# The first K block's transposes recorded ahead of the constants, and a planner that knows what large GpSimd loads cost to issue

## The chip, the core and the metric

The kernel runs on one core of one Trainium2 chip. The core has TensorE (PE, matrix products and transposes, with LDWEIGHTS shown as PEld), VectorE (DVE), ScalarE (ACT) and GpSimd (POOL); SyncE (SP) only issues DMAs here. Each engine works through its own instructions in program order and waits at semaphores for the others. The metric is the device time of one execution in microseconds. The time before is the median of 6 runs.

## The reference

The forward pass is a gated block: a layer norm, a long convolution along the sequence by an FFT, and a gated feed-forward part. The kernel returns the output and the gradients of all nine differentiable inputs.

```python
B, S, D = 1, 2048, 512        # F = 1376, shift kernel of 4 taps, bfloat16
def _fwd_reference(A_q, A_k, A_v, A_shift_k, A_ssm_k, A_ssm_D, B_x, B_w_gate, B_w_up, B_w_down):
    def _A_ref(q, k, v, shift_k, ssm_k, ssm_D):
        ...
        for t in range(ks):
            k_shift = k_shift + k_pad[:, t:t + S, :] * shift_k[:, ks - 1 - t][None, None, :]
        kv = k_shift * v
        ...
        y_f = kv_f * kf_f[None, :, :, :]        # FFTs of kv and of ssm_k, length 2 S
        y = irfft2(y_f) ...
        y = y + kv * ssm_D[None, None, :]
        return q * y
    def _B_ref(x, w_gate, w_up, w_down):
        g = jnp.einsum("bsd,df->bsf", x, w_gate)
        u = jnp.einsum("bsd,df->bsf", x, w_up)
        h = _sigmoid(g) * u
        return jnp.einsum("bsf,fd->bsd", h, w_down)
    x = A_q
    xn = _layernorm(x, axis=-1)
    s = _A_ref(xn, A_k, A_v, A_shift_k, A_ssm_k, A_ssm_D)
    g = _silu(_B_ref(xn, B_w_gate, B_w_up, B_w_down))
    return x + s * g

def reference(...):
    ...
    _out, _vjp = jax.vjp(_f, A_q, A_k, A_v, A_shift_k, A_ssm_k, A_ssm_D, B_w_gate, B_w_up, B_w_down)
    _grads = _vjp(grad_out)
```

## The kernel before

The kernel doesn't issue its instructions as it is written. `kernel_impl` calls a recorder, class `Rec`: each operation becomes a record with a running number, its dependencies worked out from the memory that it reads and writes. `Rec.order` then plans all of them with a list scheduler over a model of the machine, and `Rec.emit` (line 519, the line that the profile names for nearly everything) issues them in the planned order. In the plan each engine takes, among the records that are ready in the model, the one with the lowest number. So the place where an operation is recorded is its priority. An operation recorded with `evac` may go to ACT or to DVE, whichever the planner finds free (lines 421 to 428 and 245); it copies a PSUM tile to SBUF. The order on every engine is fixed once it is planned: if reality is later than the model, the engine waits.

Times in the model come from `cost` for engines and from `dcost` (line 331) for DMAs. `dcost` returns two numbers: how long the issuing engine is held (0.56 us for a DMA issued on POOL, 0.4 for others) and the transfer's duration, from its bytes and its shortest contiguous run. `run`, worked out in lines 338 to 346, is that run in bytes. DMAs on POOL go through software there (SWDGE), those on SP through hardware.

Four streams of work run together in the first 170 us, merged by `run_streams` (line 998): `strG`, the gate and up products of the feed-forward part, tile by tile over 16 tiles of 128 tokens; `strK`, the transform of the convolution kernel; `strV`, the shift convolution and the transform of kv; `strX`, their product and the inverse transform. K, V and X each work on four blocks (`cg`) of 128 channels. Then come the feed-forward backward pass (`stepB`), the weight gradients (`dW`) and the convolution's backward pass (`frontC`, `backC`).

The change touches the head of this. In lines 805 to 847 are recorded, in this order: the loads of the taps and of the first tile x (`ld_x`), the first K block (`ld_KT(0)`, 512 KB on SP), the weights, two more x tiles, and the k and v blocks (`ld_kv`, two loads of 512 KB on POOL for each block, in runs of 256 bytes); the column `Dcol_b` of the D taps, loaded on ACT; the broadcast of the shift taps; the identity matrix; `f_ln(SEQ[0])`, the layer norm of the first tile (statistics and a normalisation, with a power of -0.5 on POOL between); and `gen_fft_consts` (line 549), which makes the cosine tables: integer arithmetic on DVE, then three Sin on ACT, the two large ones into the halves of `Cf`, one for small tables. `f_ln(SEQ[1])` comes behind it.

`strK` (line 915) does four things for a block: it adds the D tap to column 0 of the block `KT` (one 128x1 addition on DVE), transposes `KT` in 16 pieces of 128x128 on PE into two PSUM tiles, copies each of these to `KC` (1024 columns, ACT or DVE), and then runs `step1`: products of the cosine table `Cf` with `KC`. `KT_r`, the buffer of the K block, exists once, so the load of the next block waits for the transposes. `gen_ci` transposes the cosine table itself, 32 pieces in four tiles. PSUM tiles of transposes come from banks 4 to 7 (`trA`), those of products from pairs of the eight banks (`mm2`), so they share banks.

In the V stream the accumulator `acc` (line 941) has one buffer too: four multiplications and three additions of 2048 columns on DVE fill it, it is stored to `ksh_d` by a DMA on POOL (line 953), multiplied by v, and the next block can overwrite it when the store has landed.

Of the kernel before, what the change touches and what calls it, by code (L numbers as in the profile page):

```python
# [9 lines left out]
ALU = mybir.AluOpType  # L10
# [9 lines left out]
S = 2048  # L20
# [144 lines left out]
def esize(dt):  # L165
    return 4 if dt in (f32, i32) else 2
# [16 lines left out]
class Rec:  # L183
# [147 lines left out]
    def dcost(self, alt):  # L331

        eng, meth, a, k = alt
        dst, src = a[0], a[1]
        nb = math.prod(dst.shape) * esize(dst.dtype)
        if "transpose" in meth:
            return nb / 260e3, nb / 170e3
        run = 1 << 20
        for v in (dst, src):
            dims = [d for d in v.ap if d[1] > 1]  # L340
            r = 1
            for s, n in reversed(dims if str(v.space) == "DRAM" else [d for d in v.ap[1:] if d[1] > 1]):
                if s != r:
                    break
                r *= n
            run = min(run, r * esize(v.dtype))
        if eng == "gpsimd" and run >= 256:
            run = 1024
        rate = 340e3 if run >= 2048 else 290e3 if run >= 1024 else 250e3 if run >= 512 else 150e3 if run >= 256 else run * 500
        par = dst.shape[0] if str(dst.space) != "DRAM" else src.shape[0]  # L350
        d = nb / rate
        if par < 16:
            d = min(d * 16, d + 1.0)
        return (0.56 if eng == "gpsimd" else 0.4), d

    def order(self):
        import heapq
# [185 lines left out]
def make_identity(nc, ident):  # L543
    nc.gpsimd.memset(ident, 0.0)
    nc.gpsimd.affine_select(out=ident, in_=ident, compare_op=ALU.not_equal, fill=1.0,
                            base=0, pattern=[[-1, ident.shape[1]]], channel_multiplier=1)
# [69 lines left out]
def kernel_impl(ctx, tc, A_q, A_k, A_v, A_shift_k, A_ssm_k, A_ssm_D, B_x, B_w_gate, B_w_up, B_w_down,  # L616
                grad_out, out_0, out_1, out_2, out_3, out_4, out_5, out_6, out_7, out_8, out_9):
    nc = tc.nc
# [26 lines left out]
    def ps_tr(shape, dt=bf16, name=None):  # L645
        return nc.ps(PS["tr"], shape, dt)

    ident = Ring(ar, [P]).ap
# [4 lines left out]
    Dcol_b = Ring(ar, [NG]).ap  # L653
# [42 lines left out]
    def f_ln(i, part=None):  # L696
        xj = T[i]["xq"]
        if part == 1:
            f_ln2(i)
            return  # L700
        st = T[i]["st"] = lnst.next()
        nc.vector.bn_stats(st[:, 0:6], xj)
        nc.vector.bn_aggr(st[:, 6:8], st[:, 0:6])
        nc.vector.tensor_scalar_add(st[:, 8:9], st[:, 7:8], LN_EPS)
        nc.gpsimd.tensor_tensor(out=rstd_all[:, i:i + 1], in0=st[:, 8:9], in1=neghalf, op=ALU.pow)
        if part is None:
            f_ln2(i)

    def f_ln2(i):
        xj, st = T[i]["xq"], T[i]["st"]  # L710
        nc.vector.scalar_tensor_tensor(nmr_all[:, i:i + 1], st[:, 6:7], -1.0, rstd_all[:, i:i + 1], ALU.mult, ALU.mult)
        r, b = rstd_all[:, i:i + 1], nmr_all[:, i:i + 1]
        nc.add([("scalar", "activation", (xnA[:, i, :], xj, ACT.Identity), dict(bias=b, scale=r)),
                ("vector", "tensor_scalar", (xnA[:, i, :], xj, r, b, ALU.mult, ALU.add), {})])
# [54 lines left out]
    KC_r = Ring(ar, [NJ, GW])  # L769
# [9 lines left out]
    stA = {}  # L779

    def ld_KT(cg):
        stA["KT", cg] = KT_r.next()
        nc.sync.dma_start(stA["KT", cg], A_ssm_k[cg * GW:(cg + 1) * GW, :])
# [53 lines left out]
        nc.scalar.copy(skb[:, :, db * 128:(db + 1) * 128], pb[:].rearrange("p (d t) -> p t d", t=4))  # L837
    make_identity(nc, ident)
    f_ln(SEQ[0])
    nc.gpsimd.memset(wg[:, :, F:FP], 0.0)  # L840
    nc.gpsimd.memset(wu[:, :, F:FP], 0.0)
    gen_fft_consts(nc, ar, ia, ib, negpi, Cf, BD, R)
# [21 lines left out]
    def step1(src, Qg):  # L864
        for jb in range(2):
            for c in range(2):
                ps = ps_mm([8, GW], name="ps_q")
                for jj in range(8):
                    j = jb * 8 + jj
                    nc.tensor.matmul(ps[:, jj, :], Cf[:, c, j, :], src(j), start=True, stop=True)  # L870
                nc.evac(Qg[:, c, jb * 8:(jb + 1) * 8], ps[:].rearrange("p j (g e) -> p j e g", e=4), 1024)
                yield 1024

    def flip(Qg, Qf):
        for gb in range(GQ // 8):
            pt = ps_tr([8, 128], name="ps_fl")
            for gi in range(8):
                g = gb * 8 + gi
                nc.tensor.transpose(pt[:, gi, :], Qg.rearrange("p c j e g -> p (c j e) g")[:, :, g], ident)
            nc.evac(Qf[:, gb * 8:(gb + 1) * 8, :], pt[:], 1024)  # L880
            yield 1024
# [33 lines left out]
    def strK():  # L915
        for cg in range(NG):
            KT = stA.pop(("KT", cg))
            nc.vector.tensor_tensor(KT[:, 0:1], KT[:, 0:1], Dcol_b[:, cg:cg + 1], ALU.add)
            KC = KC_r.next()
            for jh in range(2):  # L920
                pt = ps_tr([8, 128], name="ps_kt")
                for jj in range(8):
                    nc.tensor.transpose(pt[:, jj, :], KT[:, 8 * jh + jj:S:16], ident)
                nc.evac(KC[:, 8 * jh:8 * jh + 8, :], pt[:], 1024)
                yield 1024
            if cg + 1 < NG:
                ld_KT(cg + 1)
            Qg = QgK_r.next()
            yield from step1(lambda j: KC[:, j, :], Qg)
            while cg > 1 and ("s3K", cg - 2) not in flags:  # L930
                yield 0
            Qf = QfK_r.next()
            yield from flip(Qg, Qf)
            stA["QfK", cg] = Qf
            flags.add(("flK", cg))
# [32 lines left out]
    def strX():  # L968
        yield from gen_ci()
        for cg in range(NG):  # L970
# [13 lines left out]
            for qq in range(5):  # L984
# [9 lines left out]
                if qq > 0:  # L994
                    yield from inv3(ys.pop(qq - 1), qq - 1, Bg)
            yield from inv1(Bg, y2A[:, :, cg * GW:(cg + 1) * GW])

    run_streams([(gG, len(FA) * 11776, 0.05, 0.7), (strK(), 4 * 10240, 0.0, 0.7), (strV(), 4 * 16384, 0.0, 0.8),
                 (strX(), 4 * 24576 + 4096, 0.2, 1.0)])
    for r in (KT_r, KC_r, kh_r, vg_r, acc_r, term_r, kvt_r, QgK_r, QgV_r, QfK_r, QfV_r, KFg_r, Bg_r, Xc_r, Xs_r, Y_r, Ci_r):  # L1000
# [43 lines left out]
    for dst, w in ((wgT, wg), (wuT, wu)):  # L1044
        for fb in range(0, NFB, 2):
            nb = min(2, NFB - fb)
# [351 lines left out]
@with_exitstack  # L1398
def kernel(
    ctx: ExitStack,  # L1400
    tc: tile.TileContext,
    A_q: bass.AP,
    A_k: bass.AP,
    A_v: bass.AP,
    A_shift_k: bass.AP,
    A_ssm_k: bass.AP,
    A_ssm_D: bass.AP,
    B_x: bass.AP,
    B_w_gate: bass.AP,
    B_w_up: bass.AP,  # L1410
    B_w_down: bass.AP,
    grad_out: bass.AP,
    out_0: bass.AP,
    out_1: bass.AP,
    out_2: bass.AP,
    out_3: bass.AP,
    out_4: bass.AP,
    out_5: bass.AP,
    out_6: bass.AP,
    out_7: bass.AP,  # L1420
    out_8: bass.AP,
    out_9: bass.AP,
):
    kernel_impl(tc, A_q, A_k, A_v, A_shift_k, A_ssm_k, A_ssm_D, B_x, B_w_gate, B_w_up, B_w_down,
                grad_out, out_0, out_1, out_2, out_3, out_4, out_5, out_6, out_7, out_8, out_9)
# [30 lines left out]
```

## Time and profile before

| | us |
|---|---|
| median of 6 runs | 548.98 (548.06 to 552.69) |
| the profiled execution | 548.91 |
| its span, first to last instruction | 547.1 |
| PE busy | 524.1 |
| DVE busy | 457.1 |
| ACT busy | 347.1 |
| POOL busy | 150.7 |

The span is smaller than the time by 1.8 us, which lie outside the first and last instruction. An engine's busy time is the union of its instructions. PE's matmuls are pipelined and their ends are modelled. A name such as `slab<-psum` gives what an instruction writes and what it reads; `slab` is the one SBUF buffer in which everything lies, so shapes tell the operations apart. "128x1 bf16" is the D-tap addition, "128x1024 bf16<-128x1024 bf16" a copy of a tile of transposes, "128x1024 bf16<-128x1024 f32" that of a tile of products. The time in brackets behind an instruction is the engine's idle time before it, and the arrow names what ended it.

### The profile page before, as it was taken

What the parts mean: (1) busy time and instruction counts of PE and PEld (TensorE: products, weight loads), DVE (VectorE), ACT (ScalarE), POOL (GpSimd) and SP (SyncE); (2) the same over time, 40 slices, a digit from 0 to 9 for tenths busy, and PEclk for the clock granted to TensorE, in tenths of its full rate; (3) what the DMA queues carried; (4) which work ended last, traced back from release to release, by engine and by line L of the source; (5) the groups of instructions that cost most, each with busy time, mean ns of one, the idle gap of its engine ahead of it and who ended that gap; (6) DMA issues with size and microseconds to landing.
All of it is one profiled execution on the core that took longest, in us unless ns stands there. A gap on an engine that the chain in (4) does not pass through costs nothing.

```text
span 547.1 us, 13451 instructions
## 1 busy us (share of the span) xinstructions
PE 524.1 (96%) x5517; PEld 371.4 (68%) x5517; DVE 457.1 (84%) x841; ACT 347.1 (63%) x455; POOL 150.7 (28%) x260
## 2 busy tenths in 40 slices
PE   5899888999999999999999999999999999999996
PEld 3897787898688566777665676655766666665644
DVE  9699999767797998898989999829969999999550
ACT  8879899877986335544433345348777877765521
POOL 3626333304212322312222211220141051241221
PEclk9999999999999999999999999999999999999999
DMA  8999888767622999988879999999885479867422
GB/s 282 254 218 318 222 232 232 232 200 197 201 78 79 258 202 248 257 158 260 225 181 146 254 228 283 317 337 243 277 254 189 139 222 351 277 203 235 128 94 90
DMA packets 119007, 120.35 MB, mean 220 GB/s; under 512 B 76613, under 2 KB 97185, under 8 KB 118946
## 3 DMA queue, kind: packets, MB, share of 16 engines
q1 hardware_dynamic: 102514, 67.03, 49.3%
q0 software_dynamic: 15904, 52.47, 31.6%
q8 instruction: 43, 0.70, 0.5%
q14 instruction: 18, 0.15, 0.1%
q10 hardware_dynamic: 528, 0.00, 0.0%
HBM read 54.23 MB, written 47.55 MB: 186 GB/s over the span
## 4 chain that ended last, share of the span: by engine, by line
PE 71%; DVE 10%; issue 7%; ACT 4%; DMA 3%; POOL 2%; SPq 1%; POOLq 0%; DVEq 0%; ACTq 0%
PE psum L519 71%; DVE slab L519 10%; ACT slab L519 4%; DMA ksh_d<-slab 1%; POOL out_dram L519 1%; SPq L519 1%; POOL slab L519 1%; DMA dgS_d<-slab 1%; DMA slab<-hS_d 1%; ACT L519 0%; POOLq L1451 0%; POOL KK_d L519 0%; POOLq L519 0%; DVEq L519 0%; ACTq L519 0%
## 5 line engine op out<-in xcount | busy, mean ns | idle before, releaser
L519 PE MATMUL psum<-slab 128*128 128x128 bf16 (+4 forms) x5517 | 524.1, 257 | 18.0 <-ACT slab L519 11.9
L519 PEld LDWEIGHTS <-slab 128*128 128x128 bf16 (+2 forms) x5517 | 371.4, 102 | 170.4 <-issue 17.4
L519 DVE TENSOR_TENSOR slab<-slab 128x512 bf16<-128x512 bf16 (+7 forms) x467 | 300.0, 685 | 15.5 <-ACT slab L519 5.3
L519 ACT CAST slab<-psum 128x1024 bf16<-128x1024 f32 (+4 forms) x260 | 214.2, 866 | 80.3 <-PE psum L519 72.2
L519 ACT COPY slab<-psum 128x1024 bf16<-128x1024 bf16 (+2 forms) x82 | 68.5, 861 | 85.5 <-PE psum L519 85.2
L519 POOL DMA_DIRECT2D out_dram<-slab x75 | 44.9, 598 | 200.7 <-ACT slab L519 101.9
L519 DVE TENSOR_TENSOR slab<-psum,slab 128x512 bf16<-128x512 f32 (+3 forms) x84 | 63.7, 761 | 17.4 <-PE psum L519 10.0
L519 ACT ACTIVATE slab<-slab 128x512 bf16<-128x512 bf16 (+3 forms) x46 | 36.8, 805 | 18.5 <-DVE slab L519 17.9
L519 ACT ACTIVATE slab<-psum 128x512 bf16<-128x512 f32 (+1 forms) x64 | 37.3, 585 | 10.0 <-PE psum L519 8.1
L519 DVE SCALAR_TENSOR_TENSOR slab<-slab 128x1 f32<-128x1 f32 (+3 forms) x64 | 28.0, 438 | 15.7 <-ACT slab L519 12.6
L519 POOL DMA_DIRECT2D KK_d<-slab x32 | 17.3, 542 | 46.0 <-ACT slab L519 37.3
L519 DVE COPY slab<-psum 128x1024 bf16<-128x1024 bf16 (+2 forms) x34 | 21.0, 636 | 8.0 <-PE psum L519 7.7
L519 POOL DMA_DIRECT2D slab<-in_A_q_dram x29 | 16.0, 553 | 29.3 <-DMA out_dram<-slab 16.2
L519 DVE TENSOR_SCALAR slab<-slab 128x1 f32<-128x1 f32 (+7 forms) x72 | 20.5, 319 | 0.5 <-PE psum L519 0.2
L519 DVE CAST slab<-psum 128x1024 bf16<-128x1024 f32 (+1 forms) x13 | 14.8, 1141 | 4.7 <-PE psum L519 4.5
L519 DVE SCALAR_TENSOR_TENSOR slab<-psum,slab 128x512 f32<-128x512 f32 x16 | 11.0, 687 | 7.1 <-PE psum L519 6.9
L519 POOL DMA_DIRECT2D slab<-in_A_k_dram x16 | 14.9, 931 | 6.0 <-DVE slab L519 3.9
L519 POOL TENSOR_TENSOR slab<-slab 128x1 f32<-128x1 f32 x16 | 10.3, 646 | 13.6 <-DVE slab L519 13.3
L519 POOL DMA_DIRECT2D slab<-in_grad_out_dram x16 | 8.6, 539 | 19.2 <-DMA out_dram<-slab 13.1
L519 DVE BATCH_NORM_STATS2 slab<-slab 128x6 f32<-128x512 bf16 x16 | 10.9, 683 | 0.0
L519 POOL MEMSET slab<- 1x384 bf16 (+3 forms) x16 | 5.9, 376 | 14.6 <-DVE slab L519 11.2
L519 POOL DMA_DIRECT2D slab<-sF_d x7 | 3.8, 536 | 20.9 <-DVE slab L519 18.4
(21 smaller groups left out, 45.4 us busy)
## 6 DMA issues: line engine op xcount, KB each, us to landing
KK_d<-slab POOLq DMA_DIRECT2D x32, 256.0 KB, 3.9
slab<-KK_d SPq DMA_DIRECT2D x16, 512.0 KB, 6.0
out_dram<-slab POOLq DMA_DIRECT2D x58, 128.0 KB, 4.3
hS_d<-slab SPq DMA_DIRECT2D x16, 352.0 KB, 3.6
dgS_d<-slab SPq DMA_DIRECT2D x16, 352.0 KB, 4.2
duS_d<-slab SPq DMA_DIRECT2D x16, 352.0 KB, 3.5
slab<-in_A_k_dram POOLq DMA_DIRECT2D x8, 512.0 KB, 7.1
slab<-hS_d SPq DMA_DIRECT2D x8, 512.0 KB, 6.2
```

The source lines that it names most:

```text
L519: getattr(getattr(self.nc, eng), meth)(*[place(v) for v in a], **{x: place(v) for x, v in k.items()})
```

## The change

It has two parts. In the first, the D-tap addition of block 0, its 16 transposes and its two evacuations are recorded right behind `f_ln(SEQ[0])`, ahead of the constants, and `strK` leaves them out for block 0. They get lower numbers than everything in `gen_fft_consts`. The load of the second K block stays recorded in `strK`. The buffer `KC` of block 0 is taken at the new place. In `strK` block 0 no longer yields the 2 x 1024 units of work by which `run_streams` balances the streams.

In the second, `dcost` holds the issuing POOL for 1.17 us in place of 0.56 when the DMA has 600 contiguous runs or more (bytes divided by the run's bytes). This is a number in the planner's model; nothing else about these DMAs is changed.

```diff
@@ dcost
                 r *= n
             run = min(run, r * esize(v.dtype))
+        soft = 0.56 if nb < 600 * run else 1.17
         if eng == "gpsimd" and run >= 256:
             run = 1024
...
-        return (0.56 if eng == "gpsimd" else 0.4), d
+        return (soft if eng == "gpsimd" else 0.4), d
@@ kernel_impl
     make_identity(nc, ident)
     f_ln(SEQ[0])
+    nc.vector.tensor_tensor(stA["KT", 0][:, 0:1], stA["KT", 0][:, 0:1], Dcol_b[:, 0:1], ALU.add)
+    KC = stA["KC"] = KC_r.next()
+    for jh in range(2):
+        pt = ps_tr([8, 128], name="ps_kt")
+        for jj in range(8):
+            nc.tensor.transpose(pt[:, jj, :], stA["KT", 0][:, 8 * jh + jj:S:16], ident)
+        nc.evac(KC[:, 8 * jh:8 * jh + 8, :], pt[:], 1024)
     nc.gpsimd.memset(wg[:, :, F:FP], 0.0)
     nc.gpsimd.memset(wu[:, :, F:FP], 0.0)
     gen_fft_consts(nc, ar, ia, ib, negpi, Cf, BD, R)
@@ strK
             KT = stA.pop(("KT", cg))
-            nc.vector.tensor_tensor(KT[:, 0:1], KT[:, 0:1], Dcol_b[:, cg:cg + 1], ALU.add)
-            KC = KC_r.next()
-            for jh in range(2):
+            if cg > 0:
+                nc.vector.tensor_tensor(KT[:, 0:1], KT[:, 0:1], Dcol_b[:, cg:cg + 1], ALU.add)
+            KC = KC_r.next() if cg > 0 else stA["KC"]
+            for jh in range(2 if cg > 0 else 0):
                 pt = ps_tr([8, 128], name="ps_kt")
                 for jj in range(8):
                     nc.tensor.transpose(pt[:, jj, :], KT[:, 8 * jh + jj:S:16], ident)
```

## The prediction

> **What bounds the kernel now.** First the page's shares: TensorE (PE) is busy 96% of a 547.1 us span, VectorE (DVE) 84%, ScalarE (ACT) 63%. With so little idle PE, the time can fall only where PE waits, so I next asked for busy time by stage (us of each engine in each stretch).
>
> ```profile
> core 0: us, PE busy (x) PEld busy (x) DVE busy (x) ACT busy (x) POOL busy (x), PEclk, DMA share, GB/s
> ...
> 2.25:8.29 6.04, 1.86 (x4) 0.39 (x4) 6.04 (x22) 5.56 (x7) 1.51 (x6) 1.00 0.91 298
> 8.29:12.43 4.14, 3.81 (x32) 3.39 (x33) 3.86 (x19) 3.43 (x3) 1.06 (x2) 1.00 1.04 400
> 12.43:22.56 10.13, 7.91 (x130) 7.41 (x129) 7.18 (x31) 8.48 (x11) 7.78 (x8) 1.00 1.05 259
> 22.56:40.00 17.44, 17.26 (x290) 16.66 (x290) 14.79 (x26) 13.25 (x19) 5.24 (x10) 1.00 0.95 228
> 40.00:100.00 60.00, 53.35 (x776) 46.80 (x774) 57.94 (x88) 55.09 (x69) 26.03 (x43) 1.00 0.87 249
> ```
>
> See the difference of the first two numbers of a row, PE's idle time: 9.0 us before 22.56 (2.25 of it before the first matmul), 0.2 up to 40, 6.7 in 40 to 100, and, in rows not shown, 0.06 in 170 to 330. In 40 to 100 DVE is full (57.9 of 60): that stage moves with DVE. After 100 PE is the bound, with 1.0 us of idle up to 170 and some 1.3 from 330 to 541. Everything to be won lies ahead of 100 us. Next the head in order of time: start, duration, engine, operation, and in brackets the idle time before and who ended it.
>
> ```profile
> 8.29 1.89 PE L519 MATMUL psum<-slab 128*128 128x128 bf16 x16 [4.18 <-ACT slab L519]
> ...
> 10.30 0.15 DVE L519 TENSOR_TENSOR slab<-slab 128x1 bf16<-128x1 bf16 x1
> ...
> 10.51 3.65 PE L519 MATMUL psum<-slab 128*128 128x128 bf16 x44 [0.33 <-DVE slab L519]
> ...
> 14.58 1.09 PE L519 MATMUL psum<-slab 128*128 128x128 bf16 x16 [0.43 <-ACT slab L519]
> ...
> 17.34 1.15 POOL L519 DMA_DIRECT2D slab<-in_A_v_dram  x1
> 18.50 0.57 POOL L519 TENSOR_TENSOR slab<-slab 128x1 f32<-128x1 f32 x1
> 19.11 0.16 DVE L519 SCALAR_TENSOR_TENSOR slab<-slab 128x1 f32<-128x1 f32 x1 [2.38 <-POOL slab L519]
> ...
> 20.18 1.63 PE L519 MATMUL psum<-slab 128*128 128x128 bf16 x25 [0.73 <-ACT slab L519]
> ```
>
> The D-tap add is the one 128x1 bf16 add, at 10.30. The 16 K transposes follow at 10.51, at the head of the x44; the x16 at 8.29 are transposes of the cosine table, which wait for ACT's first Sin (6.23 to 8.23). At 18.50 the second tile's pow has stood behind four large loads on POOL (12.74 to 18.50), and DVE, in order, idles 2.38 us for it: the largest wait in the head that isn't for first data. PE's next gap after 20.18, 0.75 us, ends at 22.56 with ACT. In the list of waits, DVE waits for POOL twice in the whole program, 2.6 us in all.
>
> **What the Trainium skill says.** "TensorE: Matmul & The Clock Gate", Part 1: after idling TensorE runs at half clock for about 3.4 us. The trace agrees: 16 in 1.89 us at 8.29, 16 in 1.09 at 14.58. "DMA: Bandwidth & Descriptors": for a DMA issued on GpSimd software there computes the descriptors, pair by pair ("SWDGE vs HWDGE vs iDMA"), and their generation is called small and variable ("Anatomy of one DMA"). By the trace it isn't small here: a load of 2,048 runs of 256 B holds POOL 1.15 to 1.20 us, one of 128 runs 0.54 (one v load took 2.28). "Trace analysis", "Tensor Engine Instruction": ACT, DVE and GPSIMD are strict FIFO, which the 2.38 us shows.
>
> **Part 1, add and transposes recorded ahead of the constants.** No instruction is added or removed: one add (0.15), 16 transposes, two evacuations of 1024 columns (0.69 on DVE, 1.03 on ACT). A lower record number lets them go as soon as they are ready. Ready means that the K block has landed. The trace has no landing record for this load; its DMA summary has 0.65 MB moved by 5.0 us and 0.99 MB by 6.0, and what was queued ahead (4 KB), the first x tile (131 KB) and K (524 KB) make 0.66. So K is there at about 6, and the add goes into DVE's row of integer operations at about 7.0 instead of 10.30. If the landing were a microsecond later than the place, DVE would stand for it, and all constants behind: cost 0 to 1.0; I take 0, since even 6.5 is early enough.
>
> The transposes then run at 7.2, where PE is idle up to 8.29: a lead of 1.1 us, and the 0.33 before 10.51 goes too, worth about 0.2 at the cold clock. Cold time isn't saved, only moved: 1.3 us for PE. Beside that, the K buffer is freed some 3 us earlier, so that SP, which issues the second K block at 12.46 now, can do it earlier (at about 9.2, when the transposes end, or after the halo loads ahead of it on SP). That block's add stands at 20.80 now, and its transposes fill the gaps of 0.73 and 0.75 if it comes sooner. The cost is on ACT: an evacuation in its 0.73 us hole at 8.23 reaches past 8.96 and pushes the second Sin (2.00), and behind it the first tile's normalisation (10.88) and a Sin for the small tables. One evacuation pushes 0.3 to 1.0, both 1.3 to 2.1; but two evacuations then don't run at 11.69 and 12.47, so the sum by 13.5 is the same. Taken: 0.
>
> **Part 2, issue time in the model.** A DMA on POOL with at least 600 runs counts 1.17 instead of 0.56. By shapes these are the k and v loads of the forward pass (8), in the backward pass 4 k loads, 2 v loads and 4 stores of 1 MB: 18. The chip takes the same for each; only the planner's order changes. In the head it learns that four loads end 4 x 0.61 = 2.4 us later than it thought: just the 2.38 us of DVE's wait. It can't get the pow sooner (loads have lower record numbers and are ready first), but it knows that the pow is late, and will put ahead of the waiting instruction what now stands behind it: a 0.69 copy, 0.68 and 0.69 statistics, 0.18, 0.15, and the add of 0.15, together 2.5 us of work that is mostly ready. Gain for DVE: 0 to 2.4, taken 2.1. Because DVE is the bound from 40 to 100, this is carried on and comes out of the 6.7 us in which PE waits for evacuations there. After the head the model's error is 4 x 0.61 up to 66 us with 0.2 us of DVE waiting, and nothing that PE shows after 170: taken 0, as a new order by itself -1 to +4.
>
> **Sum.** 1.3 (PE in the head) + 2.1 (DVE) - 0.5 (the part of both that closes the same gaps at 20.18 and 22.56) = 2.9 us. The profiled execution took 548.91 (span 547.1 and 1.8 around it), within 0.1 of the median 548.98: 548.9 - 2.9 = 546.0. What is late next: the evacuations in 40 to 100, and the 1.5 us that PE still waits in the head for ACT.
>
> **Rivals.**
> Absorbed (548.3). The head is held by evacuations and by first loads, so that earlier transposes only wait elsewhere: the third gap (0.43), the fourth (0.31) and those at 20.18 and 22.56 all end with ACT. For it: ACT is busy 8.5 of 10.1 us there, and the normalised second tile still comes at 20.12 through POOL. Against: ACT's idle 0.73 and DVE's 2.38 us. Only half of the PE lead stays, 0.6.
>
> Slower (551.9). The place is POOL's queue in 40 to 70 us. DVE's accumulator of the V stream has one buffer, which comes free when its store to ksh_d has landed; the chain of waits runs through this (start, duration, what):
>
> ```profile
> 63.88 7.22 DMA ksh_d<-slab
> 71.12 6.15 DVE slab L519 x11
> ```
>
> With loads priced twice as high the order on POOL may put this store behind a k and a v load (1.18 + 1.18 = 2.36 us) in two or three of the blocks. DVE, full there, loses 4.7 to 7.1, less the 2.9: +1.8 to +4.2, in the middle 551.9. It decides from 2.9 us of new DVE idle in 40 to 100, and goes over 0.5% from 5.6. For it: the whole order is a greedy list, in which a small cost moves much, and the chain passes here. Against: DVE has waited only 0.5 us for that store, and better costs should on average not make a worse order.
>
> Much faster (543.9): the truer order also closes 2.1 us more of the 6.7 us of PE waiting in 40 to 100. Nothing in the profile speaks for it but that the idle time is there.
>
> **How the numbers follow.** About 0.5% (2.7 us) is what a measurement of this kernel can tell from no change. Forecast 0.40, its own range 544.5 to 547.5, somewhat over half of it beyond 546.2; much faster 0.14; absorbed 0.20; slower 0.26, nearly all beyond 551.6 or with a little under it. From these: faster 0.42, within 0.5% 0.33, slower 0.25. The range of 8 in 10 takes in the middle of the slower case and stops short of the tails: 543.3 to 552.3.
>
> **What would show it.** Right: the 128x1 add at about 7, 16 matmuls on PE before 8.2, the second K load issued before 12, no DVE wait over 1 us for POOL before 20, PE idle before 22.56 below 7.5 us, and DVE's work of the stage 40 to 100 some 2 us earlier. Wrong: an add that DVE waits for; PE idle in 40 to 100 above 7; a ksh_d store behind two loads. The forecast falls if the planner reorders the streams in 22 to 100 so that PE's idle time there changes by more than the head gives, in either direction.

## The result, and the profile after

The changed kernel took 551.5 us in the median of 33 runs, from 545.61 to 558.24; the kernel before, run beside it, 548.4 us in the median of 70 runs, most of them between 548 and 549. The ratio after to before is 1.0023, with a 95% interval from 1.001 to 1.0037: a little slower, where a little faster was forecast. The ratio leaves out runs over 1.5% above the fastest of their kernel, here the eight slowest of the 33, which is one reason why it is smaller than the ratio of the medians. The spread is itself a finding: the fastest run of the new kernel, 545.61, lies near the forecast of 546.0.

The profiled execution took 552.21 us, its span is 550.4. First the busy time by stage, in the same stretches as before.

```profile
core 0: us, PE busy (x) PEld busy (x) DVE busy (x) ACT busy (x) POOL busy (x), PEclk, DMA share, GB/s
...
2.25:8.29 6.04, 2.25 (x9) 0.79 (x9) 6.04 (x23) 5.56 (x7) 1.51 (x6) 1.00 0.92 307
8.29:12.43 4.14, 4.14 (x42) 4.14 (x41) 3.16 (x16) 3.48 (x4) 1.43 (x2) 1.00 1.04 397
12.43:22.56 10.13, 8.63 (x141) 8.38 (x140) 9.99 (x33) 8.51 (x10) 6.14 (x7) 1.00 1.00 252
22.56:40.00 17.44, 17.41 (x296) 16.86 (x293) 15.40 (x27) 15.02 (x23) 6.11 (x12) 1.00 0.98 228
40.00:100.00 60.00, 49.85 (x705) 43.52 (x702) 51.94 (x82) 50.47 (x63) 23.60 (x39) 0.94 0.89 239
100.00:170.00 70.00, 67.97 (x984) 58.81 (x983) 54.21 (x75) 59.78 (x72) 19.01 (x35) 1.00 0.60 174
```

Take again the stretch less PE's busy time. Before 22.56 PE now idles 7.5 us (2.2 + 3.8 + 0 + 1.5) where it idled 9.0: the head gained 1.5 in this execution. In the two later profiles of the same kernel, shown below, it idles 8.0 there, because the first 52 matmuls took 4.92 and 4.84 us where they take 5.70 here; so the gain is 1.0 to 1.5. DVE had 35.9 us of work behind it at 40 (the sum of its column, with 1.26 of the first stretch) where it had 33.1. Not all of these 2.7 us are a lead: by 40 the planner has given DVE two evacuations of products (2.5 us) in place of two copies (1.4 us), and over the whole program DVE is busy 459.3 us, before 457.1. But between 40 and 100 PE idles 10.15 us, before 6.65. There 3.5 us are lost, 1.1 more from 100 to 170. The head, these two and the rest make +2.6 us of idle PE over the whole span (25.6 less 23.0), and PE is busy 0.7 us longer (524.8 less 524.1): together the 3.3 us between the two profiled executions. The granted clock from 40 to 100 is 0.94, before 1.00.

The place of the largest loss is seen in PE's timeline (start, duration, operation, number; in brackets the idle time before, and what ended it).

```profile
7.83 5.70 PE L520 MATMUL psum<-slab 128*128 128x128 bf16 x52 [3.79 <-DVE slab L520]
13.70 1.05 PE L520 MATMUL psum<-slab 128*128 128x128 bf16 x16 [0.17 <-DVE slab L520]
16.08 38.22 PE L520 MATMUL psum<-slab 128*128 128x128 bf16 x623 [1.33 <-DVE slab L520]
60.30 5.90 PE L520 MATMUL psum<-slab 128*128 128x512 bf16 x45 [6.00 <-DVE slab L520]
```

From 16.08 to 54.30 PE runs without a gap that the view shows, where before it stopped at 20.18 and 22.56; then it stands 6.00 us for DVE. And DVE stands for a transfer, as the chain of waits says (start, duration, what):

```profile
26.41 10.90 DMA slab<-slab
...
37.37 4.74 DMA hS_d<-slab
42.11 0.02 issue
42.13 17.31 DMA slab<-slab
...
59.56 0.70 DVE slab L520
60.26 0.04 issue
60.30 6.02 PE psum L520 x47
```

A transfer from `slab` to `slab` is a DMA transpose here. In the gate stream each tile of h (128x1408, 352 KB) is transposed by a DMA on SP into the staging buffer `stS_r`, and from there stored to `hS_d` for the backward pass. `stS_r` exists once, h has three buffers. So the second transpose waits until the first tile's store has landed (37.37 + 4.74 = 42.11), and the product that makes the h of a tile three further on, a DVE operation, waits until the transpose has read the buffer it overwrites. Before, the same transpose was issued at 39.22 and the store behind it, which waits for it, at 45.77: at most 6.5 us. Now it takes 17.3. SP's queue of the kernel after, then of the kernel before:

```profile
37.37 0.35 SPq L520 DMA_DIRECT2D hS_d<-slab  x1
...
42.13 4.91 SPq L520 DMA_TRANSPOSE slab<-slab  x1
...
59.45 0.35 SPq L520 DMA_DIRECT2D hS_d<-slab  x1
```

```profile
36.66 0.46 SPq L519 DMA_DIRECT2D hS_d<-slab  x1
...
39.22 1.42 SPq L519 DMA_TRANSPOSE slab<-slab  x1
45.77 0.36 SPq L519 DMA_DIRECT2D hS_d<-slab  x1
```

What goes on beside it is seen in the DMA view from 36 to 62 us, in 40 slices of 0.65 us: busy share in tenths, then GB/s. First before, then after:

```profile
DMA  0099139899995789999999999999999820547699
GB/s 35 31 292 379 38 139 277 224 216 172 280 277 65 158 309 263 383 407 403 391 397 327 263 372 401 442 384 396 407 426 407 353 107 0 131 165 158 208 328 247
```

```profile
DMA  9999979998699999999999994938299999973897
GB/s 385 395 464 396 366 293 379 364 135 161 229 341 354 388 377 316 191 157 168 119 61 182 175 74 45 128 104 141 89 332 359 428 425 390 377 295 133 316 340 269
```

Before, the DMA engines are idle at 36 us and the first tile's store lands in 2.5 us; after, they are full, the store needs 4.7, and the transpose is issued at 42.13 among transfers of POOL: a k load (39.45) and stores (41.20 and 41.79) ahead of it, a v load (42.85) and stores behind it. From the 17th slice (46.4 us) to the 29th (54.9) the engines are shown busy up to 51.6 and in part after, and move 45 to 191 GB/s, on average 126, a third of the 383 of the same slices before. POOL's transfers issued behind the transpose are late too: the v load takes 13.8 us to land (9.5 before), the two stores to KK_d behind it 13.3 and 15.1 (8.9 both). These lines show what runs together; they don't tell which transfer slows which.

### The profile page after: what moved, and what is told of

Read it like the earlier page. It is cut to its first block, busy times and chain, and to the rows that moved or that the text cites. A ratio compares the mean times of both kernels' runs of the same rounds, so it can differ in the third digit from the quotient of the medians.

```text
span 550.4 us, 13452 instructions
## 1 busy us (share of the span) xinstructions
PE 524.8 (95%) x5517; PEld 372.8 (68%) x5517; DVE 459.3 (83%) x838; ACT 349.1 (63%) x458; POOL 149.2 (27%) x260
## 4 chain that ended last, share of the span: by engine, by line
PE 71%; DVE 11%; issue 6%; DMA 6%; ACT 3%; POOL 1%; POOLq 0%; ACTq 0%; DVEq 0%; SPq 0%
PE psum L520 71%; DVE slab L520 11%; DMA slab<-slab 5%; ACT slab L520 3%; POOL out_dram L520 1%; DMA hS_d<-slab 1%; POOL slab L520 0%; POOLq L1460 0%; POOLq L520 0%; ACTq L520 0%; DVEq L520 0%; SPq L520 0%; POOLq L1449 0%
## 5 line engine op out<-in xcount | busy, mean ns | idle before, releaser
L520 PE MATMUL psum<-slab 128*128 128x128 bf16 (+4 forms) x5517 | 524.8, 258 | 20.7 <-DVE slab L520 12.4
L520 DVE TENSOR_TENSOR slab<-slab 128x512 bf16<-128x512 bf16 (+6 forms) x467 | 300.3, 685 | 9.2 <-ACT slab L520 4.2
L520 ACT CAST slab<-psum 128x1024 bf16<-128x1024 f32 (+3 forms) x257 | 211.7, 863 | 83.5 <-PE psum L520 75.8
L520 ACT COPY slab<-psum 128x1024 bf16<-128x1024 bf16 (+2 forms) x85 | 71.8, 862 | 86.5 <-PE psum L520 86.3
L520 ACT ACTIVATE slab<-slab 128x512 bf16<-128x512 bf16 (+3 forms) x49 | 39.4, 807 | 16.2 <-DVE slab L520 15.6
L520 DVE SCALAR_TENSOR_TENSOR slab<-slab 128x1 f32<-128x1 f32 (+3 forms) x64 | 28.0, 438 | 13.5 <-ACT slab L520 12.6
L520 DVE COPY slab<-psum 128x1024 bf16<-128x1024 bf16 (+2 forms) x31 | 18.7, 630 | 7.7 <-PE psum L520 7.7
L520 DVE CAST slab<-psum 128x1024 bf16<-128x1024 f32 (+1 forms) x16 | 18.5, 1156 | 4.2 <-PE psum L520 3.3
L520 DVE TENSOR_SCALAR slab<-slab 128x1 f32<-128x1 f32 (+6 forms) x69 | 20.0, 341 | 0.9 <-PE psum L520 0.6
L520 POOL DMA_DIRECT2D slab<-sF_d x7 | 3.8, 536 | 19.5 <-DVE slab L520 15.1
```

What stands on the lines that cost most here:

```text
L520: getattr(getattr(self.nc, eng), meth)(*[place(v) for v in a], **{x: place(v) for x, v in k.items()})
```

## The experiments

Two things had to be told apart: which part of the change costs, and whether the late transpose is the cause of the loss or only its place. Nine variants ran, and the changed kernel was profiled twice more. Where only a few lines of the issue are edited, they follow `seq = self.order()` in `Rec.emit`, so the plan itself stays that of the kernel named. The two runs with one part alone and the one that ties evacuations to DVE are planned anew as a whole. Where an expectation gives 549.7 for the changed kernel, that is its ratio, 1.0023, times 548.4.

**One part at a time.** Part 1 alone, as a difference to the changed kernel:

```diff
-        soft = 0.56 if nb < 600 * run else 1.17
...
-        return (soft if eng == "gpsimd" else 0.4), d
+        return (0.56 if eng == "gpsimd" else 0.4), d
```

> The first part alone: add and transposes of the first K block recorded early, issue time in the model 0.56 as before. By the prediction's sum PE gains 1.3 us in the head and nothing else changes: 547.1, with PE idle before 22.56 down by about 1.3 us and DVE still waiting some 2.4 us for POOL near 19. The rival (every edit draws a new order for the whole program) allows 544 to 553, and then the difference lies behind 40 us, not in the head.

Measured 550.48 us (550.17 to 552.52), ratio 1.0041 [1.0029, 1.0053]: the first part by itself makes the kernel slower. Its head in PE's timeline:

```profile
7.82 5.32 PE L519 MATMUL psum<-slab 128*128 128x128 bf16 x52 [3.79 <-DVE slab L519]
13.69 1.05 PE L519 MATMUL psum<-slab 128*128 128x128 bf16 x16 [0.55 <-DVE slab L519]
16.07 3.40 PE L519 MATMUL psum<-slab 128*128 128x128 bf16 x57 [1.33 <-DVE slab L519]
20.51 3.70 PE L519 MATMUL psum<-slab 128*128 128x128 bf16 x62 [1.03 <-DVE slab L519]
```

PE starts at 7.82 (the forecast had it at 7.2) and runs through to 13.1. Then three gaps, 2.9 us in all, each ended by DVE, take the lead back: idle before 22.56 is 8.9 us, before 9.0. Between 40 and 100 it idles 7.95 (6.65). DVE's wait for POOL, which was expected to stay at some 2.4 us, has gone here as well: 0.6 us in the whole program, since DVE now has other work in that place.

Part 2 alone, that is the kernel before with `dcost` changed:

```diff
+        soft = 0.56 if nb < 600 * run else 1.17
...
-        return (0.56 if eng == "gpsimd" else 0.4), d
+        return (soft if eng == "gpsimd" else 0.4), d
```

> The second part alone: 1.17 us in the model for loads of 600 runs and more, the K block recorded where it was. By the prediction DVE's 2.38 us wait for POOL near 19 goes to under 0.5 and the time falls by about 2: 546.5 to 547. The rival: a new order for the whole program, 544 to 553; if the second DMA transpose again lands over 12 us after its issue, DVE waits for it and the time is 549 or more with a wide spread.

Measured 546.78 us (546.19 to 547.04), ratio 0.9966 [0.9953, 0.9979], with a spread under 1 us in five runs. DVE's timeline shows the mechanism, and below it PE's next run:

```profile
15.46 1.88 DVE L520 COPY slab<-psum 128x1024 bf16<-128x1024 bf16 x3
17.25 0.69 DVE L520 BATCH_NORM_STATS2 slab<-slab 128x6 f32<-128x512 bf16 x1
17.97 0.18 DVE L520 BATCH_NORM_AGGREGATE slab<-slab 128x2 f32<-128x6 f32 x1
19.11 0.16 DVE L520 SCALAR_TENSOR_TENSOR slab<-slab 128x1 f32<-128x1 f32 x1 [0.95 <-POOL slab L520]
```

```profile
16.05 8.14 PE L520 MATMUL psum<-slab 128*128 128x128 bf16 x142 [0.31 <-DMA slab<-in_A_ssm_k_dram]
```

The instruction that waits for POOL stands at the same 19.11, since POOL isn't faster; but a third copy and a set of statistics now stand ahead of it, and the wait has shrunk from 2.38 to 0.95 (under 0.5 was expected). PE's gaps of 0.73 and 0.75 are gone: idle before 22.56 is 7.5. The second transpose of h goes out at 38.56 and has landed at 46.7. This kernel beats both the one before and the changed one.

**Is it the second transpose?** The changed kernel with its plan, but the second tile of h stored as it is by a plain DMA, so that there is nothing to transpose:

```diff
+        tr = [o for o, *_ in seq if o.alts[0][1] == "dma_start_transpose"][1]
+        st = next(self.ops[n] for n in sorted(tr.succ) if n > 0 and self.ops[n].dma)
...
+                if op is tr:
+                    meth, a = "dma_start", (st.alts[0][2][0], a[1])
+                if op is st:
+                    continue
```

> The changed kernel with its planned order kept instruction for instruction, except that the second tile of h is stored to hS_d as it is, without the DMA transpose (that part of the gradient of w_down is then of an untransposed tile). Theory (DVE's 5.9 us wait at 53.6 is for the buffer that the late DMA transpose still reads): the wait goes, PE's 6.0 us gap with it, 545.0 (549.7 less 5 to 6 us, plus a little waited elsewhere), and the spread of the runs shrinks to that of before. Rival (the new order is worse in itself from 40 us on): another wait takes its place within the same 20 us and the time stays at 548 to 550.

Measured 546.01 us (545.77 to 549.19, seven of eight runs within 0.7), ratio 0.9961 [0.9947, 0.9975]: the loss and nearly all of the spread are gone, and POOL's transfers issued from 40 to 47 land in 5.2 to 8.9 us. This kernel also has one transfer less, so it doesn't yet tell whether the plan with the transpose in it could reach 546. The next question is what makes the transpose late.

With the v load of the third block moved behind a later store on POOL, out of the transpose's way:

```diff
...
+        late = [[s for s in pool if "A_" + w + "_dram" in name(s, 1) and s[0].alts[0][2][0].shape[0] == P][2] for w in ['v']]
+        mark = [s for s in pool if "sF_d" in name(s, 0)][3]
...
+        for s in late:
+            seq.remove(s)
+        j = seq.index(mark) + 1
+        seq[j:j] = late
```

> The changed kernel with its planned order kept, except that the 512 KB v load of the third block goes on POOL behind the fourth sF_d store (49.6 us) instead of at 42.85, so that it does not run beside the second DMA transpose. Theory (the transpose takes 17 us because POOL's burst of loads and stores from 39 to 46 us runs beside it): it lands by 53, the DVE wait falls under 2 us, 545 to 546.5. Rival (the transpose is slow because it is issued late or for what is ahead of it on SP's queue): still lands near 58, time within 1 us of the changed kernel's 549.7.

Measured 550.15 us (546.72 to 556.0, 22 runs), ratio 1.0015 [0.9997, 1.0032]. The one profiled execution, of 548.28 us, fits the theory, with a transpose from 41.87 to 48.95 and no wait; the median and the spread fit the rival. This load isn't the cause by itself.

With the second transpose writing into a spare region, so that it doesn't wait for the first tile's store (all orders unchanged):

```diff
...
+        tr, (st, *_), (st0, *_) = trs[1], dma(trs[1][0]), dma(trs[0][0])
...
+                if op is tr[0]:
+                    a = (spare.rearrange("p (a b) -> p a b", b=128), a[1])
+                if op is st:
+                    a = (a[0], spare)
```

> The changed kernel, the same instructions in the same order on every engine; only the second DMA transpose writes into a region of SBUF that is unused then, so that it doesn't wait for the store of the first one's result. Theory (the transpose is late because it is issued at 42.1, into POOL's burst, behind a store that landed at 42.1): issued near 39, landing 2 to 4 us earlier, DVE's wait of 5.9 us shrinks to 2 to 4, median 548 to 550. Rival (the place of the issue doesn't matter): median 551, spread as wide as that of the changed kernel.

Measured 547.33 us (545.81 to 548.37), ratio 0.9972 [0.9958, 0.9987]. SP's queue:

```profile
37.51 2.28 SPq L528 DMA_TRANSPOSE slab<-slab  x1
...
46.35 0.35 SPq L528 DMA_DIRECT2D hS_d<-slab  x1
```

Issued 4.6 us earlier, it lands 13 us earlier, and no gap of PE between 16 and 100 is longer than 1.4 us. The gain is larger than was expected (548 to 550). One wait on one buffer accounts for the loss: with it the median is 551.5 and the ratio 1.0023, without it 547.3 and 0.9972.

An issue after 40 us isn't enough to make the transpose slow. In the run with part 1 and the evacuations on DVE, described below, it was issued at 40.79 and its store at 44.36; there POOL issued its first load of that burst only at 43.06. With the moved v load it took at most 7.1 us from 41.87. What it runs beside matters, as far as these single executions show.

The same with the transpose also put ahead of that store on SP:

```diff
...
+        i = next(n for n, s in enumerate(seq) if s[0] is st0)
+        seq.remove(tr)
+        seq.insert(i, tr)
```

> As the run before, and the second DMA transpose also stands ahead of the first one's store on SP's queue, so that it is issued when its input is complete, at 31 to 34 us, ahead of POOL's burst of 39 to 46. Computes everything. Theory: it lands by 46, no DVE wait for it, 545.5 to 546.5 with runs as close together as those of the kernel before: ratio 0.995 to 0.997. Rival (two transposes and the same bytes only queue behind each other, or the spread has another source): median above 548.5 and runs up to 555.

Measured 547.11 us (545.94 to 549.74, 12 runs), ratio 0.998 [0.9967, 0.9992]. The transpose goes out at 32.80 and has landed by 42.5. Being still earlier brings nothing more, and the time is 1 us above what was expected. The profiled execution has no wait for it; that the rest of the spread has another source is likely, but no slow execution of this kernel was profiled.

**Does the wait make the spread?** The changed kernel itself was profiled twice more.

> The changed kernel itself, profiled once more: is the wait for the second transpose of h what makes its times spread? If so, the profiled time is 545.6 to 547 plus the time that DVE waits for this transfer between 50 and 62 us, within 1 us: some 546 when it lands by 53, 552 when it lands at 59.5. If the spread comes from elsewhere, time and this wait don't go together.

> The changed kernel a third time, with the same expectation: time equals 545.6 to 547 plus DVE's wait for the second transpose of h, within 1 us, if this wait makes the spread.

They took 550.67 and 549.81 us. DVE's wait there was 4.92 and 3.35 us, in the first profile 5.92. Time less wait is 545.8, 546.5 and 546.3: within the band expected and within 0.7 of each other, so these three don't contradict the wait as the source of the spread; the times themselves, 549.8 to 552.2, cover only part of it. The transposes were issued at 40.99 and 41.39, and their stores, at 54.12 and 56.55, show when they had landed. The last releaser is not always the same. In the third profile DVE's view names ACT, but the chain of waits has the transpose, landed 0.1 us before:

```profile
41.39 15.15 DMA slab<-slab
...
56.66 0.69 DVE L520 TENSOR_TENSOR slab<-psum,slab 128x512 bf16<-128x512 f32 x1 [3.35 <-ACT slab L520]
```

In the second profile DVE's timeline has

```profile
54.32 1.23 DVE L520 TENSOR_TENSOR slab<-slab 128x2048 bf16<-128x2048 bf16 x1 [4.92 <-DMA ksh_d<-slab]
```

which is a multiplication into the accumulator of the V stream, behind the store to ksh_d. That store was issued at 41.56 and landed at 54.30, 12.7 us later; the transpose, issued at 40.99, landed 0.2 earlier. So what is late is the whole set of transfers in flight together, and either of the two may end the wait.

**What eats the lead of part 1?** The first suspicion was the second large Sin on ACT, which in the changed kernel, as in the one with part 1 alone, comes 2.6 us later than the 8.96 of before:

```profile
8.94 1.01 ACT L520 COPY slab<-psum 128x1024 bf16<-128x1024 bf16 x1 [0.77 <-PE psum L520]
9.96 0.81 ACT L520 ACTIVATE slab<-slab 128x512 bf16<-128x512 bf16 x1
10.68 0.99 ACT L520 COPY slab<-psum 128x1024 bf16<-128x1024 bf16 x1
11.57 2.72 ACT L520 ACTIVATE slab<-slab 128x2048 bf16<-128x2048 int32 x2
```

Part 1 alone, with block 0's two evacuations given to DVE:

```diff
-        nc.evac(KC[:, 8 * jh:8 * jh + 8, :], pt[:], 1024)
+        nc.vector.tensor_copy(KC[:, 8 * jh:8 * jh + 8, :], pt[:])
```

> The first part alone, with the two evacuations of the first K block tied to DVE in place of ACT or DVE. Theory (part 1 loses its lead because these two evacuations and the first tile's normalisation go ahead of the second Sin on ACT, which starts at 11.57 in place of 8.96): Sin starts before 9.5, PE's gap of 1.33 us before 16.07 goes, PE idle before 22.56 falls from 8.9 to under 8, and the time falls from 550.5 by 1 or more. Rival (the loss lies in the order behind 40 us, whatever the head does): PE idle before 22.56 may fall, the time stays within a us of 550.5 or moves without relation to the head.

Measured 553.59 us (552.69 to 554.22), ratio 1.0087 [1.0072, 1.0101]. The Sin does start at 9.04, and yet the head is worse. The stage by busy time:

```profile
12.43:22.56 10.13, 6.59 (x70) 6.08 (x68) 8.97 (x35) 6.89 (x9) 6.95 (x9) 0.66 1.06 252
```

PE gaps of 1.94 and 1.45 us end with ACT and with DVE, and the granted clock falls to 0.66: 70 matmuls where the kernel before does 130. With a new plan and a lower clock this run doesn't isolate the Sin; the next does.

Part 1 alone once more, with nothing changed but ACT's order, the Sin ahead of both copies:

```diff
...
+        sin, to = big[1], act[act.index(big[0]) + 1]
+        seq.remove(sin)
+        seq.insert(seq.index(to), sin)
```

> Part 1 alone, as in the run with part 1 alone (550.5, 1.0041), with one instruction moved: on ACT the second large Sin is issued ahead of the two evacuations of block 0 and the first tile's normalisation, so it starts at about 9.0 again and the copies come at about 11 and 13. Theory that the pushed Sin is what ate the lead of the early transposes: PE idle before 22.56 falls from 8.9 to 7.8 or less, and the time to 548.0 to 549.2 (1.000 or a little under). Rival, that ACT and DVE have no room for two evacuations that early, whatever is put off for them: the copies now come 2 us later, PE waits for them in place of the Sin's consumers, idle before 22.56 stays at 8.5 or more, time 550 or more (1.003 or more).

Measured 551.25 us (550.71 to 555.13), ratio 1.0058 [1.004, 1.0075]. From the timelines of ACT and of PE in its profiled execution, which took 553.65:

```profile
9.04 2.00 ACT L524 ACTIVATE slab<-slab 128x2048 bf16<-128x2048 int32 x1 [0.66 <-DVE slab L524]
10.95 0.99 ACT L524 COPY slab<-psum 128x1024 bf16<-128x1024 bf16 x1
```

```profile
14.39 1.07 PE L524 MATMUL psum<-slab 128*128 128x128 bf16 x16 [0.67 <-DVE slab L524]
16.77 3.40 PE L524 MATMUL psum<-slab 128*128 128x128 bf16 x57 [1.31 <-DVE slab L524]
21.20 2.97 PE L524 MATMUL psum<-slab 128*128 128x128 bf16 x49 [1.03 <-DVE slab L524]
```

The Sin is back in its place, the copies follow it, and the gaps of 1.3 and 1.0 us stand as they were, 0.7 us later. PE idles 9.5 us before 22.56. The same move with both parts and the transpose freed from its store:

> Both parts, the second transpose of h freed from the wait for the store (547.3, 0.9972 without more), and the second large Sin ahead of block 0's two evacuations on ACT. Sin theory: about 1 us better than that, 546.0 to 546.5 (0.9945 to 0.996). Rival (no room for the evacuations): 547.3 or more (0.997 and above).

Measured 548.2 us (546.04 to 553.57, 22 runs), ratio 0.9997 [0.9976, 1.0018], no better than without the move, and with a wide spread that its one profile, at 548.39 and without a PE gap over 1.5 us between 16 and 100, doesn't explain. In both cases the rival held: delaying the Sin isn't what the early evacuations cost. In the run with part 1 alone DVE is busy 9.83 us of the 10.13 from 12.43 to 22.56, before 7.18, and 2.45 of the difference are two evacuations of products (128x1024 from f32), where ACT did the first ones before in 1.01 us each. The part 1 run, then the kernel before:

```profile
12.41 1.22 DVE L519 CAST slab<-psum 128x1024 bf16<-128x1024 f32 x1 [0.91 <-PE psum L519]
...
14.79 1.23 DVE L519 CAST slab<-psum 128x1024 bf16<-128x1024 f32 x1
```

```profile
13.52 1.01 ACT L519 CAST slab<-psum 128x1024 bf16<-128x1024 f32 x1
```

PE's gaps at 13.69 and 16.07 end within 0.1 us of their ends. That the planner's new split of these evacuations is the price is argued from this; no run tried the old split.

## Why the prediction was wrong

The forecast said 546.0 us; the median was 551.5, inside the range, and the ratio is on the slower side by less than half a percent.

**The head.** For both parts together the total came near the number, though not in the way that was forecast. The add ran at 7.63 (about 7 was said), so PE started at 7.83, a lead of 0.46 us where 1.1 was forecast, and five of the 16 transposes came before 8.29, where all 16 were to come before 8.2. The second K load was issued at 9.78 (before 12, as said), but the add of that block came at 21.95, later than the 20.80 of before, so it filled no gap. DVE waits for POOL 0.2 us in the whole program (no wait over 1), and PE idles 7.5 to 8.0 us before 22.56. The sum was put together wrongly: 1.3 for part 1 and 2.1 for part 2 were added, less 0.5 for the gaps that both close. The runs of single parts give +1.9 us (550.48 less the 548.58 that the kernel before took beside it) and -1.8. Part 2 alone has the whole gain of PE in the head, 7.5 us of idle time. And each part alone shortens DVE's waits for POOL, 2.6 us in the whole program before, 0.6 with part 1 and 1.6 with part 2: the two gains share one hole.

**Part 1, the step "Taken: 0" for ACT.** It failed. "The sum by 13.5 is the same" looked only at ACT's own total, and it put an evacuation into ACT's hole at 8.23. The transposes came too late for that: the first evacuation starts at 8.94, and both go ahead of the Sin together with the normalisation, which pushes it by 2.6 us. With part 1 alone PE's lead at 7.82 is paid back in three gaps by 22.56, and more is lost up to 100. But the Sin, which the step named as what is pushed, is not what costs: restored to its place it brought nothing.

**Part 2.** Right in mechanism and about right in size: 2.1 us of filling work were forecast, and DVE's wait fell from 2.38 to 0.95 in the run with this part alone, whose time is 1.8 us lower. But this run is also a new plan for the whole program, and a part of the 1.8 may come from that.

**The step that decided: "After the head ... taken 0, as a new order by itself -1 to +4".** This is where the direction was lost. The new order issues the second transpose of h 1.8 to 2.9 us later than before into a denser set of transfers, and the wait in that place makes a gap on PE of 3.4 to 6.0 us in the three profiles. The term that was taken as 0 measures some 4 us in the medians, 2.4 to 2.8 by the ratios: 551.5 less the 547.3 and 547.1 of the two kernels that keep all transfers and don't wait for that buffer. Less DVE's wait the three times are 545.8 to 546.5, and without the transpose the kernel measured 546.0. That this equals the forecast is in part luck: the kernel without the transpose has a transfer less, and part 1's share of the forecast gain didn't come. The middle of the term should not have been 0 for a program with a single-buffered DMA round in that stage. The trace of before did show what was needed: a store and a transpose in series on SP, at 36.66, 39.22 and 45.77, in a stage where DVE has no slack. The prediction examined POOL's queue in that stage and never SP's.

**The rivals.** The slower one gave 551.9, and its price and its stage (40 to 70 us) are right, its mechanism half. It named DVE's wait for the store to ksh_d; in one of three profiles exactly this ended the wait. But it put the delay into POOL's queue, behind two loads. The store stands behind one load there and is issued at 41.56, 1.4 us earlier than before; it is the transfer that takes 12.7 us (7.4 before), beside the transpose. The sign that would topple the forecast, PE's idle time between 22 and 100 changing by more than the head gives, is what came in the first two profiles: +3.4 against -1.5 and +2.3 against -1.0 (in the third +0.8 against -1.0). "Absorbed" describes part 1 alone in the head, and "much faster" nothing.

What stays open: which of the transfers in flight together slow the others, and why by so different amounts from one execution to the next; why part 1 alone loses a further 1.3 us between 40 and 100 (its trace has PE gaps of 1.77 us at 62.13, ended by DVE, and of 1.41 at 81.31, ended by ACT, and no late transpose); and why two variants with the transpose freed still spread over 3.8 and 7.5 us.

## What to carry to other kernels

When a planner re-orders everything behind an edit, list the DMA rounds with a single buffer (transfer, store, transfer again) in the stages that have no slack, and ask of each who waits when it comes 3 us later; price that, not zero. Two gains that fill the same gaps are not to be added. An evacuation moved forward is free only if the engine that takes over what it displaces has room, which a sum of busy time of one engine doesn't show. A correction of the cost model paid here, and moving work by hand did not: the correction alone, 0.9966, is the version to keep.

## What the runs showed of the hardware

A DMA transpose within SBUF of 352 KB (128x1408, bf16) took from 3.5 to 17.3 us to land within the same program. The Trainium skill, "DMA: Bandwidth & Descriptors", "Latency and other measured facts", gives an effective 261 GB/s for DMA transposes with a non-contiguous middle dimension, measured on one kernel, and about 350 to 400 for contiguous ones; 352 KB at 261 would be an estimated 1.4 us. Our times run from issue to landing, beside other traffic, so the two are not quite the same quantity, but no run here came near that estimate: the quickest is 2.5 times as long, and the measurement decides. In the first profile of the changed kernel, while the late transpose and POOL's loads and stores were in flight together, both were slow, and from 46.4 to 54.9 us the engines moved 45 to 191 GB/s.

A stop of PE can cost clock as well as time. After the 6.00 us stop the granted clock was 0.50 from 60 to 64 us, where the kernel before has 1.00; in the other two profiles of the changed kernel it was 0.57 from 56 to 60 after the gap of 3.67 us, and 0.50 from 57.4 to 62.5 after that of 3.42. After the 1.33 us gap before 16.08 it could go either way. In the first profile of the changed plan the clock stayed at 1.00, with 141 matmuls from 12.43 to 22.56; in those of the kernels with the untransposed tile and with the moved v load there were 113, at a granted clock of 0.83, with the same order on PE up to there. Of the kernel with the untransposed tile this execution took 549.19 us, where its others took 545.8 to 546.5. What decides between the two isn't shown here.
